# Decoding 64-bit weights in 8 pieces of 512 columns, one step per block

## The chip, the cores and the metric

The kernel runs on one core of one Trainium2 chip. The metric is the device time of one execution in microseconds (us). A core has a matrix engine (TensorE, PE in the profile; its weight loads are PEld), a vector engine (VectorE, DVE), an activation engine (ScalarE, ACT), a general engine (GpSimd, POOL) and a queue engine (SyncE, SP), from which this kernel issues all its transfers. They run side by side and wait for each other by semaphores. Each works through its own instructions strictly in the order in which the program lists them.

## The reference

Three stages follow each other on an input `x` of 8 batches x 3072 points x 256 features:

```python
X = rfft(x, axis=1)                       # stage 1: spectrum of every batch
Yr = Xr @ w_r - Xi @ w_i + b_r            #   complex mix of the features
Yi = Xr @ w_i + Xi @ w_r + b_i
y = irfft(soft_threshold(Yr, Yi, 0.01))
logits = y @ phi                          # stage 2: soft mixture, 8 experts x 4 slots
slots = softmax_over_points(logits).T @ y
z = softmax_over_slots(logits) @ relu(slots @ w1) @ w2   # expert by expert
h = z @ w_in                              # stage 3: 256 -> 1024 -> 256
u = h * softmax(h)
out = (layer_norm(u) * g_ln) @ w_out
```

`w_in` (256 x 1024) and `w_out` (1024 x 256) are products of a float32 array and a NumPy float64 scalar, so they arrive as 64-bit floats. The chip's engines work on 32-bit values. So the kernel takes each 64-bit number as two 32-bit integers, `lo` and `hi`, and builds the float32 from them with integer operations on VectorE.

## The kernel before

**Stages.** Phase 1 handles the spectrum, the mix and the slot sums of all batches. Phase 2 runs the experts and then the third stage over 192 tiles of 128 points. The change touches phase 1 alone.

**Blocks.** The main loop of phase 1 goes over 96 blocks: 8 batches of 12 groups of frequencies, `i = 12 b + t`. One turn of the loop lists, in this order:

1. `s1_next`: one part of the first transform stage of the next batch, in the first nine blocks of a batch. TensorE writes `s`, ScalarE copies it to `asb`, ScalarE and GpSimd split the next chunk of `x` into a high and a low part (`xsplit`, L224 on ScalarE, L225 on GpSimd). The result goes to DRAM (`ad`) and comes back as `apt`.
2. a `tick()`
3. `stage2` of block i + 1: four groups of matmuls into `xps`, two ScalarE copies (L285, L286), then VectorE's `xsum` (L287) and `xl` (L288). In blocks with even t, the load of a later `apt` is put on a list of delayed steps here.
4. a `tick()`, then `s1_next` and the transposes of block i - 2, then a `tick()`
5. `mix` of block i: matmuls into `pb` and `pa`, then VectorE's L329, L330 and L332, then GpSimd's L333, which finishes the soft threshold.
6. `stage2s` of block i + 1 (ScalarE L302, VectorE L303), then a `tick()`

**The narrow path.** Everything else of phase 1 (logits, the maxima, the softmaxes, the slot sums) is a chain of small steps. A step calls `after(n, fn)` to have the next one listed n ticks later, and `tick()` lists the steps that are due. There are four ticks in a block.

**The decoding.** `decode` lists the load of one piece, 128 partitions x 256 numbers of 8 bytes, into `raw` (L623). It hands ten VectorE operations (L630 to L639) to the delayed list, one per tick, the first one seven ticks later. Two ticks behind the last comes `dec_out`, a store of the 256 float32 columns into `win_dram` or `wout_dram` (L646). The tiles `raw`, `da`, `db` and `dm` exist once each. There are 16 pieces, and the loop starts one at the end of every fifth block (i = 4, 9, ..., 79). So the ten operations of the piece started at the end of block i lie behind the L303 of block i + 2 (the first), in blocks i + 3 and i + 4, and at the first tick of block i + 5 (the last). Counted from one L329 to the next, three stretches in a row hold operations of a piece, and the next two hold none.

**Where the results are needed.** The decoded weights are read back from DRAM at the end of phase 1 (`wo`, L133) and in phase 2 (`wi`, L811).

Of the kernel before, what the change touches and what calls it, by code (L numbers as in the profile page):

```python
# [8 lines left out]
F32 = mybir.dt.float32  # L9
F32R = mybir.dt.float32r  # L10
I32 = mybir.dt.int32
I64 = mybir.dt.int64
AF = mybir.ActivationFunctionType
ALU = mybir.AluOpType
# [4 lines left out]

# how many quarters of a block later each step of the narrow path is issued  # L20
LAG = dict(
    csoft_last=16, head=4, split0=3, load_x=3, a_out=0, qt=5, qtr=3, e2=3, r_x=2, inv1=3, mx=0, ltr=1, maxt=2, maxb=4,
    dsub=0, dexp=2, csoft=5, fwd1=4, rescale=3, rexp=3, csoft2=3, csoft3=5, c_x=4, c_out=1, dtr=3, d_x=3, fwd2=4,
    sums4=0, slots=1, sums=4, dec=7,
)
# [7 lines left out]
def kernel(  # L33
# [40 lines left out]
    ones = glob.tile([128, 128], F32, name="ones")  # L74
# [22 lines left out]

    # w1 and some of w2 in halves of 4 KB, the first ones where the chunks of x have been;
    # the rest of w2 in quarters where the spectra of the last batches have been
    w1t, w2t = {}, {}  # L100
# [35 lines left out]

    # ------------------------------------------------------------------ spectrum
    def phase1(pl: ExitStack, pr_: ExitStack):
# [25 lines left out]
        d2_sb = k_p.tile([128, 24, 128], F32, name="d2_sb")  # L164
        # [-(wr + wi) | wi - wr | wr]
        wc_h = k_p.tile([128, 2, 768], F32R, name="wc_h")
# [7 lines left out]

        # steps of the narrow path are put off by quarters of a block, so that what they wait for has ended
        heap = []
# [11 lines left out]

        # x loads and the first transform stage
        xt = {}  # L190
# [76 lines left out]
        def stage2(b, t):  # L267
            q, tq = divmod(t, 4)
            a = apt[b, q, tq // 2]
            ps = psx.tile([128, 2, 2, 2, 64], F32, name="xps", tag="xps")  # L270
            for gp in range(2):
                for dh in range(2):
                    mm(
                        ps[:, dh, :, gp, :],
                        a[:, gp, tq % 2, dh * 128:(dh + 1) * 128],
                        d2_sb[:, 8 * q + 2 * tq + gp, :].rearrange("p (c j) -> p c j", c=2),
                    )
            hi = xt_p.tile([128, 2, 2, 128], F32R, name="xh", tag="xh")
            lo = xt_p.tile([128, 2, 2, 128], F32R, name="xl", tag="xl")
            xi = xt_p.tile([128, 2, 128], F32, name="xi", tag="xi", bufs=1)  # L280
            sm_ = xt_p.tile([128, 2, 128], F32, name="xsum", tag="xsum", bufs=1)
            sh = xt_p.tile([128, 2, 128], F32R, name="sh", tag="sh")
            sl = xt_p.tile([128, 2, 128], F32R, name="sl", tag="sl")
            psv = ps.rearrange("p a c g j -> p a c (g j)")
            ACT.activation(out=xi, in_=psv[:, :, 1, :], func=AF.Copy)  # L285
            ACT.activation(out=hi, in_=psv, func=AF.Copy)  # L286
            DVE.tensor_tensor(out=sm_, in0=psv[:, :, 0, :], in1=xi, op=ALU.add)  # L287
            DVE.tensor_tensor(out=lo, in0=psv, in1=hi.bitcast(F32), op=ALU.subtract)  # L288
            if t == 0:
                # the first slot holds the two real frequencies: wr alone acts on both  # L290
                xd = xt_p.tile([128, 2, 1], F32, name="xd", tag="xd", bufs=1)
                DVE.tensor_tensor(out=xd, in0=xi[:, :, 0:1], in1=psv[:, :, 0, 0:1], op=ALU.subtract)
                DVE.tensor_copy(out=sm_[:, :, 0:1], in_=psv[:, :, 0, 0:1])
                DVE.tensor_copy(out=xd_h[:, :, 0:1], in_=xd)
                DVE.tensor_tensor(out=xd_l[:, :, 0:1], in0=xd, in1=xd_h[:, :, 0:1].bitcast(F32), op=ALU.subtract)
                for z in (hi, lo):
                    DVE.tensor_copy(out=z[:, :, :, 0:1], in_=zero4)
            xhl[b, t] = (hi, lo, sh, sl, sm_)
# [101 lines left out]

        # (part, n2) x (g, s) to (part, g) x (n2, s): one 32 x 32 block for each slot
        def r_x(b, z):
# [77 lines left out]

        # the running maximum of each column, and what it makes of the sums so far and of this batch's
        def rescale(b):
# [28 lines left out]

        # slots to the partitions; the points (row j, 8 m + a) in the order (a, j, m)
        def c_x(b, c, z):
# [76 lines left out]

        # the mean of g * w_out over the features
        def gmean(z):
# [26 lines left out]

        # decoding the 8 byte weights  # L620
        def decode(src, dst):
            raw = raw_p.tile([128, 256], I64, name="raw", tag="raw")
            SP.dma_start(out=raw, in_=src)  # L623
            v = raw.bitcast(I32).rearrange("p (n two) -> p n two", two=2)
            lo, hi = v[:, :, 0], v[:, :, 1]
            a = raw_p.tile([128, 256], I32, name="da", tag="da")
            c = raw_p.tile([128, 256], I32, name="db", tag="db")
            m = raw_p.tile([128, 256], I32, name="dm", tag="dm")
            ops = [
                lambda: DVE.tensor_scalar(out=a, in0=hi, scalar1=3, scalar2=0x7FFFFFF8, op0=ALU.logical_shift_left, op1=ALU.bitwise_and),  # L630
                lambda: DVE.scalar_tensor_tensor(out=a, in0=lo, scalar=29, in1=a, op0=ALU.logical_shift_right, op1=ALU.bitwise_or),
                lambda: DVE.scalar_tensor_tensor(out=a, in0=hi, scalar=_s32(0x80000000), in1=a, op0=ALU.bitwise_and, op1=ALU.bitwise_or),
# [3 lines left out]
                lambda: DVE.tensor_scalar(out=c, in0=a, scalar1=_s32(0xFF800000), scalar2=None, op0=ALU.bitwise_and),  # L636
                lambda: DVE.tensor_scalar(out=m, in0=lo, scalar1=0x1FFFFFFF, scalar2=None, op0=ALU.bitwise_and),
                lambda: DVE.scalar_tensor_tensor(out=c.bitcast(F32), in0=m, scalar=2.0**-52, in1=c.bitcast(F32), op0=ALU.mult, op1=ALU.mult),
                lambda: DVE.tensor_tensor(out=a.bitcast(F32), in0=c.bitcast(F32), in1=a.bitcast(F32), op=ALU.add),  # L639
            ]  # L640
            for k, op in enumerate(ops):
                after(LAG["dec"] + k, op)
            after(LAG["dec"] + len(ops) + 1, dec_out, dst, a.bitcast(F32))

        def dec_out(dst, f):
            SP.dma_start(out=dst, in_=f)  # L646

        # constants
        dft = sm_p.tile([96, 96], F32, name="dft", tag="qt_sb", bufs=2)
# [88 lines left out]
        decs = []  # L738
        for k in range(2):
            for h in range(4):  # L740
                decs.append((w_in[128 * k:128 * k + 128, 256 * h:256 * h + 256], win_dram[128 * k:128 * k + 128, 256 * h:256 * h + 256]))
        for k in range(8):
            decs.append((w_out[128 * k:128 * k + 128], wout_dram[128 * k:128 * k + 128]))

        for i in range(B * NT):
# [4 lines left out]
            if i + 1 < B * NT:  # L750
                stage2(*divmod(i + 1, NT))
                if t % 2 == 0:
                    k = i // 2 + 2
# [11 lines left out]
            tick()  # L765
            if decs and i % 5 == 4:
                decode(*decs.pop(0))
        st_transpose(B - 1, NT - 2)
# [10 lines left out]

    # ------------------------------------------------------------------ experts and the second block  # L780
    def phase2(p2: ExitStack, pw: ExitStack):
# [6 lines left out]

        # the slots' weights of a third of a batch, the same in the four groups of partitions
        def load_c(b, h):  # L790
# [11 lines left out]

        # the slots: the column groups added up, turned over
        ps = pt.tile([128, 2, 32], F32, name="pslt", tag="pt")
# [10 lines left out]

        # experts: four at a time in the column groups
        so = t_p.tile([128, 2, D], F32, name="so")
# [46 lines left out]
        for fh in range(2):  # L864
            for dh in range(2):
                mm(pg[fh], sot[:, dh].rearrange("p k s -> p (k s)"), wi[:, dh, 512 * fh:512 * fh + 512], dh == 0, dh == 1)
        # rows: high part twice, then low part twice
        for fh in range(2):
# [17 lines left out]

        # rows: high, low, high, low parts of the weights of 4 tiles
        def pieces(j):
# [13 lines left out]

        # the negated first product
        def hmat(i):
# [61 lines left out]

        # sum of (F u - sum u)^2
        def vari(i):
# [17 lines left out]

        # (F^3 (sum e + 1e-9)^2 1e-6 + variance sum) ** -0.5
        def rstd(j, k):
# [7 lines left out]
        def outp(i):  # L996
# [9 lines left out]
            if j == NG - 1:  # L1006
                # nothing left to wait for: each tile on its own
                rstd(j, slice(k, k + 1))
# [57 lines left out]

# [1 line left out]
def _consts():  # L1068
# [114 lines left out]
```

## Time and profile before

| | |
|---|---|
| three runs | 1517.56, 1522.68, 1522.99 us; median 1522.68 us |
| the profiled execution | 1519.0 us from its first to its last instruction; no other time is recorded for it |
| blocks 0 to 95 | L329 of block 0 at 43.8 us, of block 95 at 636.6 us |
| VectorE busy, whole span | 1267.1 us (83%) |
| TensorE busy, whole span | 1432.5 us (94%) |
| decoding operations | 160 on VectorE, 16 loads of 256 KB, 16 stores of 128 KB |

The span runs from the first instruction to the last. It lies among the three runs. Busy times are sums over one engine, and the engines overlap, so they don't add up to the span. A row of the trace names the line of the kernel, the engine, the operation, and its output and inputs by the program's names.

### The profile page before, as it was taken

Reading aid. Unit: us, or ns where it says so; the run is one execution under the profiler, and the core shown is the slowest. Engines: PE = TensorE matmul, PEld = TensorE weight load, DVE = VectorE, ACT = ScalarE, POOL = GpSimd, SP = SyncE. Lnnn points to the kernel's source line nnn. Section 1 sums busy time; section 2 is a strip of 40 time slices with the busy share of each in tenths; the row PEclk is TensorE's granted clock in tenths of the full one; section 3 lists DMA queues with packets and bytes.
Section 4 is the critical chain, followed back from the end, with each engine's and each line's share of the span. In section 5 each row is a group of like instructions: output and inputs, shape, how many; then the busy total and the mean of one; then the engine's idle time right before and its main releaser. Section 6 shows DMA issues by size and latency. Waiting matters only on the chain.

```text
span 1519.0 us, 31798 instructions
## 1 busy us (share of the span) xinstructions
PE 1432.5 (94%) x12300; PEld 1299.6 (86%) x12300; DVE 1267.1 (83%) x1981; ACT 1064.7 (70%) x2169; POOL 669.0 (44%) x703
## 2 busy tenths in 40 slices
PE   6998889989989999977999999999999999999999
PEld 3887777878778778745999999999999999999998
DVE  6698879998989898845888888888888888888886
ACT  5655564655555553423888888888888888888887
POOL 5545554645464543332334433433443344334432
PEclk8999999999999999988999999999999999999999
DMA  9955363626454551194111111111111111111001
GB/s 269 280 146 166 93 180 86 188 80 178 112 161 124 157 178 57 26 336 145 43 43 56 51 49 43 57 42 43 43 59 54 43 46 53 43 42 57 29 29 43
DMA packets 81383, 149.17 MB, mean 98 GB/s; under 512 B 9360, under 2 KB 46992, under 8 KB 81232
## 3 DMA queue, kind: packets, MB, share of 16 engines
q1 hardware_dynamic: 81232, 147.15, 31.3%
q8 instruction: 96, 1.57, 0.4%
q14 instruction: 55, 0.45, 0.1%
HBM read 91.55 MB, written 55.57 MB: 97 GB/s over the span
## 4 chain that ended last, share of the span: by engine, by line
PE 70%; DVE 17%; DMA 5%; issue 4%; ACT 2%; POOL 2%; SPq 0%; DVEq 0%; ACTq 0%; POOLq 0%
PE po L86 36%; PE pu L89 11%; PE hps L86 6%; PE pb L86 4%; PE s L86 3%; PE pm L86 3%; PE xps L86 2%; DMA xc<-in_x_dram 2%; DVE yb L330 2%; PE pa L86 2%; DVE yb L329 1%; DVE xl L288 1%; DVE sl L303 1%; DVE dm_sb L559 1%; DVE dm L634 1%
## 5 line engine op out<-in xcount | busy, mean ns | idle before, releaser
L923 DVE TENSOR_REDUCE st<-hps 128x1 f32<-128x1024 f32 x192 | 235.1, 1225 | 119.2 <-PE hps L86 119.2
L333 POOL TENSOR_TENSOR s<-yb,s 128x512 f32<-128x512 f32 x95 | 132.3, 1393 | 263.7 <-DVE s L332 227.0
L964 DVE TENSOR_TENSOR ul<-pu,uh 128x512 fp32r<-128x512 f32 x384 | 246.5, 684 | 0.8 <-ACT uh L956 0.8
L938 DVE SCALAR_TENSOR_TENSOR u<-hps,e 128x1024 f32<-128x1024 f32 x192 | 233.3, 1215 | 2.1 <-ACT e L930 2.1
L86 PE MATMUL po<-gw_h,uh 128*128 128x256 f32 x1536 | 230.3, 293 | 0.0
L973 ACT ACTIVATE sq<-u,st 128x1024 f32<-128x1024 f32 x192 | 224.4, 1169 | 0.0
L930 ACT ACTIVATE e<-hps,st 128x1024 f32<-128x1024 f32 x192 | 213.1, 1110 | 2.9 <-DVE st L923 2.9
L86 PE MATMUL po<-gw_l,uh 128*128 128x256 f32 x1536 | 213.5, 282 | 0.0
L86 PE MATMUL po<-gw_h,ul 128*128 128x256 f32 x1536 | 212.9, 280 | 0.0
L956 ACT ACTIVATE uh<-pu 128x512 fp32r<-128x512 f32 x384 | 208.7, 603 | 2.7 <-PE pu L89 2.7
L89 PEld LDWEIGHTS pu<-ident,u 128*128 128x128 f32 x1536 | 179.8, 140 | 26.0 <-DVE ul L964 0.6
L89 PE MATMUL pu<-ident,u 128*128 128x128 f32 x1536 | 199.9, 273 | 0.0
L86 PEld LDWEIGHTS po<-gw_h,ul 128*128 128x128 f32 x1536 | 196.2, 189 | 0.0
L86 PEld LDWEIGHTS po<-gw_h,uh 128*128 128x128 f32 x1536 | 195.7, 190 | 0.0
L86 PEld LDWEIGHTS po<-gw_l,uh 128*128 128x128 f32 x1536 | 195.6, 189 | 0.0
L225 POOL TENSOR_TENSOR x<-xc,x 96x512 fp32r<-96x512 f32 x120 | 161.9, 1360 | 37.1 <-ACT x L224 35.5
L1017 POOL TENSOR_TENSOR os<-osb,st 128x1024 f32<-128x1024 f32 x47 | 89.1, 1895 | 180.9 <-issue 173.2
L1012 ACT ACTIVATE osb<-po 128x256 f32<-128x256 f32 x188 | 72.2, 384 | 113.9 <-PE po L86 113.9
L898 POOL TENSOR_TENSOR c<-ct,c 32x512 fp32r<-32x512 f32 x96 | 123.2, 1283 | 6.7
L86 PE MATMUL hps<-gst,c 128*128 128x512 f32 x384 | 120.0, 394 | 5.8 <-DVE u L938 4.3
L993 POOL TENSOR_TENSOR st<-st 128x4 f32<-128x4 f32 (+1 forms) x51 | 10.1, 198 | 255.1 <-ACT sq L973 255.0
L86 PE MATMUL s<-x,df_h 96*96 96x512 f32 x240 | 105.6, 442 | 17.6 <-ACT asb L251 6.0
(191 smaller groups left out, 2693.5 us busy)
## 6 DMA issues: line engine op xcount, KB each, us to landing
apt<-ad SPq DMA_DIRECT2D x96, 256.0 KB, 4.1
out_dram<-os SPq DMA_DIRECT2D x47, 512.0 KB, 2.6
xc<-in_x_dram SPq DMA_DIRECT2D x56, 384.0 KB, 3.9
ad<-asb SPq DMA_DIRECT2D x56, 384.0 KB, 3.5
ct<-c_dram SPq DMA_DIRECT2D x96, 128.0 KB, 2.7
wt<-in_moe_w_dram SPq DMA_DIRECT2D x21, 512.0 KB, 9.3
ws<-in_moe_w_dram SPq DMA_DIRECT2D x22, 256.0 KB, 5.8
xc<-in_x_dram SPq DMA_DIRECT2D x16, 192.0 KB, 5.0
```

The costliest lines, as they stand in the source:

```text
L86: PE.matmul(out=out, lhsT=lhsT, rhs=rhs, start=start, stop=stop)
L89: PE.transpose(out=out, in_=in_, identity=ident[0:k, 0:k])
L225: POOL.tensor_tensor(out=lo, in0=t, in1=hi.bitcast(F32), op=ALU.subtract)
L333: (DVE if (b, t) == (B - 1, NT - 1) else POOL).tensor_tensor(out=s, in0=yb, in1=s, op=ALU.subtract)
L898: POOL.tensor_tensor(out=c4[z], in0=src[z], in1=c4[z].bitcast(F32), op=ALU.subtract)
L923: DVE.tensor_reduce(out=st[:, 0, k:k + 1], in_=hps[i], op=ALU.min, axis=AX.X)
L930: ACT.activation(out=e, in_=hps[i], func=AF.Exp, bias=st[:, 0, k:k + 1], scale=-1.0, accum_out=st[:, 1, k:k + 1])
L938: DVE.scalar_tensor_tensor(out=u, in0=hps.pop(i), scalar=1.0, in1=et.pop(i), op0=ALU.mult, op1=ALU.mult, accum_out=st[:, 2, k:k + 1])
L956: ACT.activation(out=uh[:, 4 * hf:4 * hf + 4, :], in_=ut[i, hf], func=AF.Copy)
L964: DVE.tensor_tensor(out=ul[:, 4 * hf:4 * hf + 4, :], in0=ut.pop((i, hf)), in1=uht[i][0][:, 4 * hf:4 * hf + 4, :].bitcast(F32), op=ALU.subt ...
L973: ACT.activation(out=sq, in_=ut.pop(i), func=AF.Square, bias=st[:, 2, k:k + 1], scale=-float(DFF), accum_out=st[:, 3, k:k + 1])
L1017: POOL.tensor_tensor(out=os2, in0=o, in1=q, op=ALU.mult)
```

## The change

The weights are decoded in 8 pieces of 128 x 512 numbers. A piece of `w_out` holds two groups of 128 rows. `raw` is now 4 KB per partition, and the three work tiles are 2 KB each.

A piece takes eight VectorE operations. The two that moved the top three bits of `lo` into the result and masked them out of `lo` are gone. The operation that adds the low part now takes all of `lo`, read as an unsigned integer.

The delayed list is no longer used for the decoding. `dec_step` is called once per block from i = 4 on, right behind `stage2`, and lists one operation. Its first call lists the load of the first piece alone. Behind the eighth operation of a piece, the same call lists the store of the piece and the load of the next. So piece n (0 to 7) has its operations in blocks 5 + 8n to 12 + 8n, and the last operation lies in block 68.

```diff
         def decode(src, dst):
-            raw = raw_p.tile([128, 256], I64, name="raw", tag="raw")
-            SP.dma_start(out=raw, in_=src)
...
+            raw = raw_p.tile([128, 512], I64, name="raw", tag="raw")
+            a = raw_p.tile([128, 512], I32, name="da", tag="da")
...
+            lo = raw.bitcast(U32).rearrange("p (n two) -> p n two", two=2)[:, :, 0]
...
+            SP.dma_start(out=r, in_=src)
...
-                lambda: DVE.scalar_tensor_tensor(out=a, in0=lo, scalar=29, in1=a, op0=ALU.logical_shift_right, op1=ALU.bitwise_or),
...
-                lambda: DVE.tensor_scalar(out=m, in0=lo, scalar1=0x1FFFFFFF, scalar2=None, op0=ALU.bitwise_and),
-                lambda: DVE.scalar_tensor_tensor(out=c.bitcast(F32), in0=m, scalar=2.0**-52, in1=c.bitcast(F32), op0=ALU.mult, op1=ALU.mult),
+                lambda: DVE.scalar_tensor_tensor(out=c.bitcast(F32), in0=lo, scalar=2.0**-52, in1=c.bitcast(F32), op0=ALU.mult, op1=ALU.mult),
                 lambda: DVE.tensor_tensor(out=a.bitcast(F32), in0=c.bitcast(F32), in1=a.bitcast(F32), op=ALU.add),
-            ]
-            for k, op in enumerate(ops):
-                after(LAG["dec"] + k, op)
-            after(LAG["dec"] + len(ops) + 1, dec_out, dst, a.bitcast(F32))
+                lambda: dec_out(dst, f),
+            ])
+
+        def dec_step():
+            if not dec_ops and decs:
+                decode(*decs.pop(0))
+                return
+            if dec_ops:
+                dec_ops.pop(0)()
+                if len(dec_ops) == 1:
+                    dec_ops.pop(0)()
+                    if decs:
+                        decode(*decs.pop(0))
...
             if i + 1 < B * NT:
                 stage2(*divmod(i + 1, NT))
+                if i > 3:
+                    dec_step()
                 if t % 2 == 0:
...
             tick()
-            if decs and i % 5 == 4:
-                decode(*decs.pop(0))
```

## Rows read from the trace of the kernel before

**Rows 1.** The page: two engines' busy time, and the chain that ended last

```profile
PE 1432.5 (94%) x12300; PEld 1299.6 (86%) x12300; DVE 1267.1 (83%) x1981; ACT 1064.7 (70%) x2169; POOL 669.0 (44%) x703
...
PE 70%; DVE 17%; DMA 5%; issue 4%; ACT 2%; POOL 2%; SPq 0%; DVEq 0%; ACTq 0%; POOLq 0%
```

**Rows 2.** Busy time by stage: stretch, its length, then each engine's busy time

```profile
200.00:300.00 100.00, 91.65 (x882) 79.09 (x881) 92.80 (x159) 59.87 (x134) 55.18 (x41) 0.98 0.52 146
400.00:500.00 100.00, 90.48 (x861) 76.35 (x859) 90.80 (x164) 55.28 (x124) 50.38 (x37) 0.98 0.41 117
760.00:1519.00 759.00, 755.52 (x6139) 731.48 (x6137) 638.14 (x896) 644.44 (x1260) 309.93 (x415) 1.00 0.13 46
```

**Rows 3.** The same, twelve stretches of two blocks without decoding operations, and their sum

```profile
core 0: us, PE busy (x) PEld busy (x) DVE busy (x) ACT busy (x) POOL busy (x), PEclk, DMA share, GB/s
...
251.18:264.68 13.50, 13.03 (x128) 10.33 (x127) 12.35 (x30) 6.87 (x16) 7.27 (x5) 1.00 0.18 55
283.64:292.26 8.62, 8.62 (x91) 7.97 (x93) 8.21 (x15) 6.74 (x15) 6.19 (x6) 1.00 0.91 245
314.97:325.89 10.92, 10.88 (x104) 9.64 (x96) 9.86 (x17) 6.94 (x18) 4.62 (x3) 1.00 0.53 158
...
482.65:496.06 13.41, 11.99 (x130) 9.03 (x130) 12.47 (x26) 6.44 (x14) 5.51 (x4) 1.00 0.35 109
...
549.83:560.86 11.03, 11.03 (x141) 10.21 (x141) 9.47 (x18) 6.86 (x16) 4.86 (x4) 1.00 0.78 258
sum 141.86, PE 135.68 PEld 116.76 DVE 110.33 ACT 90.11 POOL 79.29; mean PE 11.31 PEld 9.73 DVE 9.19 ACT 7.51 POOL 6.61
```

**Rows 4.** The same, sum over the twelve stretches of three blocks between them

```profile
sum 258.17, PE 230.39 PEld 197.10 DVE 249.18 ACT 138.66 POOL 125.97; mean PE 19.20 PEld 16.43 DVE 20.76 ACT 11.55 POOL 10.50
```

**Rows 5.** VectorE operations by line: durations in ns, least, median and greatest

```profile
L630 DVE TENSOR_SCALAR da<-raw x16: 1367/1380/1397, 74.4 to 563.1; 128x256 int32<-128x256 int32 x16
L632 DVE SCALAR_TENSOR_TENSOR da<-raw,da x16: 396/418/1201, 78.1 to 565.8; 128x256 int32<-128x256 int32 x16
L637 DVE TENSOR_SCALAR dm<-raw x16: 261/280/289, 84.9 to 576.1; 128x256 int32<-128x256 int32 x16
L639 DVE TENSOR_TENSOR da<-db,da x16: 358/932/1507, 88.8 to 581.9; 128x256 f32<-128x256 f32 x16
```

**Rows 6.** VectorE groups by line and shape: sum in us, mean in ns

```profile
L329 DVE TENSOR_TENSOR yb<-pb,bias 128x512 f32<-128x512 f32 x96 | 65.5, 682 | 18.5 <-PE pb L86 16.9 <-POOL x L225 0.6 <-POOL dt_sb L530 0.5
L332 DVE TENSOR_SCALAR s<-yb 128x512 f32<-128x512 f32 x96 | 42.6, 443 | 3.9
L303 DVE TENSOR_TENSOR sl<-xsum,sh 128x256 fp32r<-128x256 f32 x96 | 42.0, 437 | 2.3 <-ACT sh L302 2.3
```

**Rows 7.** The timeline around one L634: start in us, duration in us, engine

```profile
302.50 1.39 POOL L333 TENSOR_TENSOR s<-yb,s 128x512 f32<-128x512 f32 x1 [2.88 <-DVE s L332]
302.67 1.38 DVE L634 TENSOR_SCALAR dm<-db 128x256 int32<-128x256 int32 x1
```

**Rows 8.** The timeline at the ends of the first and last of 66 L288

```profile
59.97 1.30 POOL L225 TENSOR_TENSOR x<-xc,x 96x512 fp32r<-96x512 f32 x1
60.15 0.68 DVE L288 TENSOR_TENSOR xl<-xps,xh 128x512 fp32r<-128x512 f32 x1
...
481.54 2.02 POOL L496 TENSOR_TENSOR c_sb<-lg_sb,rm 96x1024 f32<-96x1024 f32 x1 [1.49 <-DVE rm L494]
482.05 0.67 DVE L288 TENSOR_TENSOR xl<-xps,xh 128x512 fp32r<-128x512 f32 x1
```

**Rows 9.** The queue: issue times of loads and stores (ns), landing times (us)

```profile
L623 SPq DMA_DIRECT2D raw<-in_moe_w_in_dram x8: 423/458/1367, 59.7 to 283.7; - x8
...
DMA to landing us min/median/max: 2.7/4.6/8.1
...
L646 SPq DMA_DIRECT2D win_dram<-da x8: 319/337/759, 89.3 to 313.6; - x8
...
wt<-in_moe_w_dram SPq DMA_DIRECT2D x6, 512.0 KB, 7.0
```

More of the change, by code (lines that the diff above doesn't have):

```diff
@@ L12 @@
 I64 = mybir.dt.int64
+U32 = mybir.dt.uint32
 AF = mybir.ActivationFunctionType
@@ L23 @@
     dsub=0, dexp=2, csoft=5, fwd1=4, rescale=3, rexp=3, csoft2=3, csoft3=5, c_x=4, c_out=1, dtr=3, d_x=3, fwd2=4,
-    sums4=0, slots=1, sums=4, dec=7,
+    sums4=0, slots=1, sums=4,
 )
@@ L618, in sums @@
                 after(1, slots, b)
+        dec_ops = []
         def decode(src, dst):
-            raw = raw_p.tile([128, 256], I64, name="raw", tag="raw")
-            SP.dma_start(out=raw, in_=src)
+            raw = raw_p.tile([128, 512], I64, name="raw", tag="raw")
+            a = raw_p.tile([128, 512], I32, name="da", tag="da")
+            c = raw_p.tile([128, 512], I32, name="db", tag="db")
+            m = raw_p.tile([128, 512], I32, name="dm", tag="dm")
             v = raw.bitcast(I32).rearrange("p (n two) -> p n two", two=2)
[L625 to L629, printed above, removed]
+            hi = v[:, :, 1]
+            lo = raw.bitcast(U32).rearrange("p (n two) -> p n two", two=2)[:, :, 0]
+            r = raw if len(src.shape) == 2 else raw.rearrange("p (k d) -> p k d", k=2)
+            SP.dma_start(out=r, in_=src)
+            f = a.bitcast(F32) if len(src.shape) == 2 else a.bitcast(F32).rearrange("p (k d) -> p k d", k=2)
+            dec_ops.extend([
                 lambda: DVE.tensor_scalar(out=a, in0=hi, scalar1=3, scalar2=0x7FFFFFF8, op0=ALU.logical_shift_left, op1=ALU.bitwise_and),
-                lambda: DVE.scalar_tensor_tensor(out=a, in0=lo, scalar=29, in1=a, op0=ALU.logical_shift_right, op1=ALU.bitwise_or),
                 lambda: DVE.scalar_tensor_tensor(out=a, in0=hi, scalar=_s32(0x80000000), in1=a, op0=ALU.bitwise_and, op1=ALU.bitwise_or),
@@ L739, in phase1 @@
         for k in range(2):
[L740 to L743, printed above, removed]
+            for h in range(2):
+                decs.append((w_in[128 * k:128 * k + 128, 512 * h:512 * h + 512], win_dram[128 * k:128 * k + 128, 512 * h:512 * h + 512]))
+        for k in range(0, 8, 2):
+            z = slice(128 * k, 128 * k + 256)
+            decs.append((w_out[z].rearrange("(k p) d -> p k d", p=128), wout_dram[z].rearrange("(k p) d -> p k d", p=128)))
         for i in range(B * NT):
```

## Prediction

> **What bounds the kernel now.** I began with the page. TensorE is busy for 94% of the span and VectorE for 83%, and the chain that ended last lies 70% on TensorE and 17% on VectorE [rows 1]. Such shares are means over stages with different limits, so the second view is busy time by stage. In phase 2, from 760 us on, TensorE works 755.5 of 759 us [rows 2]; nothing there changes. In the middle of phase 1 both engines are near the top: TensorE 91.65 and 90.48 of 100 us, VectorE 92.80 and 90.80 [rows 2]. Two engines at 91% may mean that each bounds some of the blocks, so the third view separates them.
>
> The decoding comes in a rhythm of five blocks: three stretches from L329 to L329 hold its operations, two hold none. I took blocks 24 to 83. Sixty is a multiple of both five and twelve, so every place t of a batch falls equally often on each beat, and the two kinds of block differ by decoding alone. Twenty-four blocks without it last 141.86 us, 5.911 us each; VectorE works 110.33 us in them, 4.597 each and 78% of the time, TensorE 135.68 us, 96% [rows 3]. Thirty-six blocks with it last 258.17 us, 7.171 each; VectorE works 249.18 us, 97%, TensorE 89% [rows 4]. So VectorE sets the pace where there is decoding, and TensorE, or the chain through it, elsewhere. A piece stretches three blocks by 1.260 us each, 3.78 us in all. The same windows say how: a piece brings 249.18 - 36 x 4.597 = 83.7 us of VectorE work over 12 pieces, 6.97 us each; the 1.314 us per block in which VectorE would have idled take up 3 x 1.314 = 3.94, and the remaining 3.03 must show as time. 3.78 is seen.
>
> **Why the old operations are dear.** L637 takes 261 to 289 ns, and L630, also one input and 256 columns, never less than 1367 [rows 5]. L630, L634 and L638 are listed at the last tick of a block, behind L332, whose end releases GpSimd's L333. The timeline shows the consequence: L333 runs from 302.50 to 303.89, and L634, begun at 302.67, ends at 304.05, just behind it [rows 7]. So an operation of this kind beside a GpSimd operation lasts until that one ends.
>
> The page "SBUF — State Buffer" of the Trainium skill, section "Who interferes with whom", states this as an exclusive lock: a tensor_scalar in a two-port mode, or a VectorE operation with two inputs in SBUF, and a GpSimd operation that reads SBUF block each other whole, in order of issue. The rule also cuts the other way: a decoding step that comes first would hold up GpSimd; that is the second rival below. By the row alone only the VectorE wait of 1.1 us counts.
>
> **The change part by part.**
>
> *Removed: the old decoding.* All 16 pieces go: 16 x 3.78 = 60.5 us less on the path. This applies the mean of twelve pieces to all.
>
> *Added: 64 operations of 512 columns.* Four are tensor_scalar; L332, that form at 512, takes 443 ns [rows 6]. It reads adjacent words, while two of the new ones read every other word as L637 does; L637's 280 at 256 columns [rows 5] shows no penalty. Three are scalar_tensor_tensor: L632 takes 418 at 256 [rows 5], and 256 more columns cost 682 - 437 = 245 ns by L329 against L303 [rows 6], so 663. One is a tensor_tensor: 358 at the least for L639 [rows 5], plus 245, 603. Together 4 x 443 + 3 x 663 + 603 = 4364 ns a piece, 546 an operation. Reading `lo` as unsigned has no row; nothing dearer than the 663 of its neighbours is assumed.
>
> To this comes waiting for GpSimd. At the new place, the end of L288, I read for 66 blocks (5 to 70, by the L288 in them) how long a GpSimd operation still ran. The first of these L288 ends at 60.83 with 0.44 us of L225 left, the last at 482.72 with 0.84 us of L496 left [rows 8]; with VectorE's next start some 0.07 us before the recorded end, 33 of 66 are covered at all, and the mean over all 66 is 0.34 us. The floor is 0, the ceiling 1.1 us, as for L630 [rows 5]. I take 0.34: 0.89 us an operation, 57 us of VectorE work in all, against 16 x 6.97 = 112.
>
> *How much of 0.89 us is on the path.* A block without decoding leaves VectorE 1.314 us, so on average it fits. The idle time is uneven, though. Of the twelve two-block stretches five have less than 2 x 0.89 = 1.78 us: 1.15, 0.41, 1.06, 0.94 and 1.56 [rows 3]. They lack 0.63, 1.37, 0.72, 0.84 and 0.22, 3.78 us over 24 blocks, 0.16 a block. That is too kind, since idle time need not lie where the step is. The old response is the other end: 3.78 us of time per 6.97 us of work, 0.54, times 0.89, 0.48 a block. I take the middle, 0.32: 64 x 0.32 = 20.5 us, with 10 and 31 as ends; the whole 57 is a rival's.
>
> *Moved: the reload.* Before, a piece's load had over two blocks to land. Now the store and the next load are listed behind the last step, and the first step of the next piece is listed one block later. It needs the new `raw`, and, since it writes `da`, the end of the store. On the queue the store is issued in 0.34 us and the load in about 0.43 [rows 9]. The old 256 KB loads land in 2.7, 4.6 and 8.1 us (least, median, greatest), and 512 KB of another tensor in 7.0 [rows 9]; at the 117 to 146 GB/s of these stretches [rows 2], 256 KB more take 1.8 to 2.2 us if they get that whole rate, less if the mean leaves room. I estimate 6.2 us. The step is due a block of 6.2 us later, less its predecessor's own 0.66, so about 5.5. VectorE waits 0.34 + 0.43 + 6.2 - 5.5 = 1.5 us, of which the 0.4 us left idle absorb a part: 1.1 us, eight times, 9 us. The first load stands alone in front of block 5, in batch 0, and is counted as one of the eight. Floor: 2.7 + 1 + 0.77 comes before 5.5, nothing. Ceiling: 8.1 + 2 + 0.77 - 5.5 = 5.4 us each, 43 in all.
>
> Behind the waiting step on VectorE stand the L329, L330 and L332 of its block and L303, behind L332 GpSimd's L333. TensorE can still run that block's mix, as its inputs were made one block earlier, but the next mix needs `pb` emptied by L329. That is why an absorbed part is credited and a hidden whole is not.
>
> *The queue.* The store now waits on SP for the eighth operation, and the load behind it goes out at once. Behind both stand the `apt` loads listed at the next tick, at most one step late, for a tile whose `stage2` comes three blocks on. So nothing is added for them. The cover is those blocks; without it, seven delays of about one step, 0.9 us, would cost 6 us. Bytes are the same, in half as many transfers.
>
> *Ends earlier.* The last operation lies in block 68, not 84. This is contained in the sum, which removes all old work and adds 64 operations.
>
> **The sum.** The profiled execution has a span of 1519.0 us and no separate time; the median of the runs is 1522.7, 3.7 more, which I leave outside the change. 1522.7 - 60.5 + 20.5 + 9 = 1491.7, about 1491 us; in terms of the span, 1488.
>
> **The rivals.**
>
> *Hidden whole.* If the steps fall into idle time and no load is late, only the 60.5 us remain: 1462. For it: 1.314 us idle a block against 0.89. Against it: the five tight stretches, and the ceiling of the loads.
>
> Beside it stands the rule in "Perfetto Trace Analysis" of the Trainium skill, section "Identifying the Most-Contended Engine", that matmul busy time is a poor measure and weight-load busy time a better one. By it TensorE would have 116.76 of 141.86 us, 82%, and the undecoded block would not be at its floor; a block at VectorE's 4.597 + 0.89 = 5.49 us would take the 64 blocks a further 64 x 0.42 = 27 us down, to 1435. This trace speaks against it only in that blocks with 78% VectorE still last 5.9 us.
>
> *The cover is gone.* If a step that starts first holds GpSimd back, L225 and L333 come late, and with them the next part of the first stage. Then each step costs its 0.89 us even where VectorE idles: 1522.7 - 60.5 + 57 + 9 = 1528, within 0.5% of before. Against it: GpSimd is only 55% busy at 200 to 300 us and 50% at 400 to 500 [rows 2].
>
> *TensorE is the floor everywhere.* If TensorE at 91% were the limit, VectorE's relief would be worth nothing: 1522. Against it: blocks without decoding are 1.26 us shorter at the same TensorE work [rows 3, 4].
>
> *Slower: the reload sets the pace.* Eight waits must give back 60.5 - 20.5 = 40 us, and 7.6 more for 0.5%, so over 6.0 us each on the path, a landing of about 11 us or more. At 8 us each: 1522.7 - 60.5 + 20.5 + 64 = 1547. For it: three of the eight loads (blocks 12, 36 and 60) fall on t = 0, where the next batch's transfers begin; one stretch without decoding shows the transfer engines 91% busy [rows 3]. Against it: no old load took over 8.1 us [rows 9].
>
> **Chances.** 0.5% is 7.6 us, about what a measurement of this kernel can tell from no change. The forecast has 0.70, hidden whole 0.13 (0.03 of it below 1458), cover gone 0.06, TensorE 0.04, the reload 0.07. Faster by over 0.5%: the first two, 0.83. Within it: 0.10. Slower: 0.07. The forecast's own range follows from 10 to 31 us for the steps and 0 to 24 for the waits: 1472 to 1517. To hold 8 in 10 I extend it down past hidden whole and leave the tail of the waits and the three slower cases out: 1458 to 1515.
>
> **What would show it.** VectorE's busy time falls by about 112 - 57 = 55 us; less than 30 would mean that waits for GpSimd are commoner. The new tensor_scalars should be near 0.44 us and the two-input ones near 0.66, half of them lengthened. Blocks 24 to 68 should last 6.2 us, blocks 69 to 83 5.9. The first operation of a piece should start with 1 to 2 us of idle time put down to the load or the store. If those idle times are over 6 us, the fourth rival holds; if blocks 69 to 83 last as long as before, the third does.

## The result and the profile after

The changed kernel takes 1477.99 us, the median of four runs (1475.65 to 1480.34), against 1522.84 us before in the same comparison. The ratio is 0.9721, with a 95% interval of 0.970 to 0.9743: 2.8% or 45 us faster. The profiled execution took 1476.49 us with a span of 1474.7 us.

Nearly all of it is won in phase 1. L330, which is L329 of the kernel before one line further down, comes in block 95 at 593.4 us (before: 636.6) and in block 0 at 42.1 (43.8). So 41.5 of the 44.3 us between the two spans lie between blocks 0 and 95. Another 1.7 us lie ahead of block 0, where neither kernel has decoded anything, and can't be put down to the change. From the page, the lines that answer to [rows 1]:

```profile
PE 1422.3 (96%) x12300; PEld 1293.8 (88%) x12300; DVE 1192.1 (81%) x1885; ACT 1065.2 (72%) x2169; POOL 671.9 (46%) x703
...
PE 76%; DVE 11%; DMA 7%; issue 3%; ACT 2%; POOL 1%; SPq 0%; DVEq 0%; ACTq 0%; POOLq 0%
```

VectorE works 75 us less, and its share of the chain falls from 17% to 11%, while TensorE's rises from 70% to 76%. The decoding operations of the changed kernel, by line and shape (VectorE's groups: busy us, mean ns, then idle time in front and what ended it), to be read against [rows 5, 6]:

```profile
L641 DVE SCALAR_TENSOR_TENSOR da<-da,dm 128x512 int32<-128x512 int32 x8 | 9.6, 1202 | 0.0
L644 DVE TENSOR_TENSOR da<-db,da 128x512 f32<-128x512 f32 x8 | 6.7, 836 | 0.0
L638 DVE SCALAR_TENSOR_TENSOR da<-raw,da 128x512 int32<-128x512 int32 x8 | 6.3, 789 | 0.0
L637 DVE TENSOR_SCALAR da<-raw 128x512 int32<-128x512 int32 x8 | 6.0, 753 | 6.2 <-DMA raw<-in_moe_w_in_dram 3.1 <-DMA raw<-in_moe_w_out_dram 3.1
L640 DVE TENSOR_SCALAR dm<-db 128x512 int32<-128x512 int32 x8 | 5.9, 740 | 0.0
L643 DVE SCALAR_TENSOR_TENSOR db<-raw,db 128x512 f32<-128x512 uint32 x8 | 5.5, 683 | 0.0
L642 DVE TENSOR_SCALAR db<-da 128x512 int32<-128x512 int32 x8 | 4.8, 595 | 0.0
L639 DVE TENSOR_SCALAR db<-raw 128x512 int32<-128x512 int32 x8 | 3.5, 442 | 0.0
```

They add up to 48.3 us, a mean of 755 ns over 64. The ten old groups add up to 137.7 us over 160 operations; half of that lies in three of the ten:

```profile
L638 DVE SCALAR_TENSOR_TENSOR db<-dm,db 128x256 f32<-128x256 int32 x16 | 24.1, 1509 | 0.0
L634 DVE TENSOR_SCALAR dm<-db 128x256 int32<-128x256 int32 x16 | 22.1, 1380 | 0.0
L630 DVE TENSOR_SCALAR da<-raw 128x256 int32<-128x256 int32 x16 | 22.1, 1380 | 0.0
```

In the changed kernel the first operation of a piece waits for its load, 6.2 us in all.

The operations of the changed kernel by line, with least, median and greatest duration:

```profile
L637 DVE TENSOR_SCALAR da<-raw x8: 427/639/1280, 63.2 to 401.6; 128x512 int32<-128x512 int32 x8
L638 DVE SCALAR_TENSOR_TENSOR da<-raw,da x8: 677/682/1118, 68.1 to 408.3; 128x512 int32<-128x512 int32 x8
L639 DVE TENSOR_SCALAR db<-raw x8: 417/418/578, 74.8 to 415.3; 128x512 int32<-128x512 int32 x8
L644 DVE TENSOR_TENSOR da<-db,da x8: 658/856/1060, 97.3 to 445.9; 128x512 f32<-128x512 f32 x8
```

The undisturbed operation is seen at the least or the median: 0.42 us for a tensor_scalar and 0.66 to 0.68 for those with two inputs. Busy time in blocks 24 to 68, which hold steps, and 69 to 83, which hold none (columns as in [rows 3]):

```profile
171.52:451.44 279.92, 268.15 (x2579) 231.56 (x2578) 228.38 (x422) 173.79 (x389) 161.13 (x118) 0.99 0.53 153
451.44:541.95 90.51, 88.71 (x874) 76.04 (x873) 71.74 (x141) 53.74 (x120) 45.70 (x34) 1.00 0.46 143
```

A block with a step lasts 279.92 / 45 = 6.22 us, and one without 90.51 / 15 = 6.03.

### The profile page after: what moved, and what is told of

The parts are those of the page before. It is cut to its first block, busy times and chain, and to the rows that moved or that the text cites. A ratio compares the mean times of both kernels' runs of the same rounds, so it can differ in the third digit from the quotient of the medians.

```text
span 1474.7 us, 31675 instructions
## 1 busy us (share of the span) xinstructions
PE 1422.3 (96%) x12300; PEld 1293.8 (88%) x12300; DVE 1192.1 (81%) x1885; ACT 1065.2 (72%) x2169; POOL 671.9 (46%) x703
## 4 chain that ended last, share of the span: by engine, by line
PE 76%; DVE 11%; DMA 7%; issue 3%; ACT 2%; POOL 1%; SPq 0%; DVEq 0%; ACTq 0%; POOLq 0%
PE po L87 37%; PE pu L90 11%; PE hps L87 6%; PE pb L87 6%; PE s L87 3%; PE pm L87 3%; PE xps L87 3%; PE pa L87 2%; DMA xc<-in_x_dram 2%; DMA ad<-asb 2%; PE sps L90 1%; DVE yb L330 1%; DVE yb L331 1%; DVE xl L289 1%; DVE dm_sb L560 1%
## 5 line engine op out<-in xcount | busy, mean ns | idle before, releaser
L334 POOL TENSOR_TENSOR s<-yb,s 128x512 f32<-128x512 f32 x95 | 132.2, 1391 | 223.5 <-DVE s L333 208.5
L226 POOL TENSOR_TENSOR x<-xc,x 96x512 fp32r<-96x512 f32 x120 | 164.8, 1381 | 41.2 <-ACT x L225 37.4
L252 ACT ACTIVATE asb<-s 96x512 f32<-96x512 f32 x112 | 66.7, 596 | 82.7 <-PE s L87 72.2
```

Of the source, the lines that this page charges most:

```text
L226: POOL.tensor_tensor(out=lo, in0=t, in1=hi.bitcast(F32), op=ALU.subtract)
L334: (DVE if (b, t) == (B - 1, NT - 1) else POOL).tensor_tensor(out=s, in0=yb, in1=s, op=ALU.subtract)
```

## The experiments

**The theory.** The old decoding cost time in two ways: 160 small operations, and places at which three in ten of them always stood beside a GpSimd operation. Eight pieces of 512 remove the first and the new place the second. What is left, some 22 us, is one step a block that VectorE cannot hold in its idle time, plus waits for loads. **Rivals:** size alone gives the gain and the place is worth nothing; place alone gives it; the decoding was hidden, so that the floor is near 1478.

Medians of runs on the same chip are compared. Before is 1519.9 us beside the first four runs below, 1520.4 beside the next four and 1520.7 beside the last four.

**One operation a piece.**

```diff
-            dec_ops.extend([
...
-                lambda: dec_out(dst, f),
-            ])
+            dec_ops.append(lambda: DVE.tensor_scalar(out=a, in0=hi, scalar1=0x007FFFFF, scalar2=0x3F000000, op0=ALU.bitwise_and, op1=ALU.bitwise_or))
+            dec_ops.extend([lambda: None] * 7)
+            dec_ops.append(lambda: dec_out(dst, f))
```

> The changed kernel with one VectorE operation a piece left instead of eight, in the same block as before the first of them; loads, stores and their places unchanged. Left out: the decoding itself (the weights of the third stage are other numbers). My sum: the steps cost 0.32 us a block, so 56 fewer give 18 us back: about 1460. Rival (the old decoding cost more than the 60.5 us that I took off, and the steps cost as I said or more): the floor is lower than 1522.7 - 60.5 = 1462 although loads and stores remain; by batch 6 of the changed kernel, which has no steps (70.0 us against 75.0 in batches 2 to 4), 0.42 us a block, about 1454. Rival (hidden whole): 1476 to 1478.

Measured: 1457.65 us (1454.36 to 1459.16), ratio 0.9591 (0.9567 to 0.9615), between the 1460 of the sum and the 1454 of the first rival. The floor lies below 1462, so hidden whole falls. The 20 us between 1458 and 1478 are the price of 56 steps together with most of the waiting for loads, which falls from 6.2 to 0.5 us in front of the one operation left:

```profile
L636 DVE TENSOR_SCALAR da<-raw 128x512 int32<-128x512 int32 x8 | 7.1, 882 | 0.5 <-DMA raw<-in_moe_w_in_dram 0.5
```

**The step at the end of the block.**

```diff
-                if i > 3:
-                    dec_step()
...
                 stage2s(*divmod(i + 1, NT))
+                if i > 3:
+                    dec_step()
```

> The changed kernel with the step (and the store and load behind the eighth) listed at the end of a block, behind L304, instead of behind the second transform stage. If the place makes the old operations dear (GpSimd's soft-threshold operation has just been released there), each step lasts some 1.4 to 1.8 us instead of 0.75, VectorE gets about 60 x 0.9 = 55 us more work, and half or so shows as time: 1495 to 1520. Rival (the place is worth nothing, it was fewer and longer operations that gained): within 5 us of the changed kernel.

Measured: 1504.3 us (1501.99 to 1506.6), ratio 0.9895 (0.9872 to 0.9917). The same 64 operations, and 26 us more than the changed kernel. Two of them by line, and then the timeline around L643:

```profile
L638 DVE SCALAR_TENSOR_TENSOR da<-raw,da 128x512 int32<-128x512 int32 x8 | 14.2, 1772 | 0.0
L640 DVE TENSOR_SCALAR dm<-db 128x512 int32<-128x512 int32 x8 | 12.1, 1514 | 0.0
```

```profile
301.10 1.28 POOL L226 TENSOR_TENSOR x<-xc,x 96x512 fp32r<-96x512 f32 x1 [0.27 <-ACT x L225]
...
306.62 1.39 POOL L334 TENSOR_TENSOR s<-yb,s 128x512 f32<-128x512 f32 x1 [2.48 <-DVE s L333]
306.80 1.77 DVE L643 SCALAR_TENSOR_TENSOR db<-raw,db 128x512 f32<-128x512 uint32 x1
307.98 1.74 POOL L226 TENSOR_TENSOR x<-xc,x 96x512 fp32r<-96x512 f32 x1
```

L638 takes 1772 ns here and 789 in the changed kernel. GpSimd's L334 ends at 308.01, and L643 ends 0.56 us later: it waited, then ran. All eight groups add up to 95.4 us against 48.3. GpSimd is held up in turn: the L226 that begins at 307.98, beside L643, takes 1.74 us, the one at 301.10 1.28. Over the whole execution the 39 L226 that begin while a decoding operation runs take 1.62 us on average, the other 81 take 1.33.

**New pieces in the old places**, one operation per tick, a piece every ten blocks.

```diff
...
+            for k, op in enumerate(ops):
+                after(7 + k, op)
+            after(7 + len(ops) + 1, dec_out, dst, f)
...
-                if i > 3:
-                    dec_step()
...
+            if decs and i % 10 == 4:
+                decode(*decs.pop(0))
```

> The pieces of 512 with eight operations, but listed as in the kernel before: one operation per tick through the delayed list, a piece every ten blocks. If size and count of the operations bring the gain: near 1478. If the place and the even spread do: the eight operations of a piece press into two blocks, two of them (the first and the fifth) behind L333 in GpSimd's shadow; by the old response of 0.54 us per us of work, with 8 x (4.4 + 2.2 + 1) = 61 us of work, 33 us against the 20.5 + 9 of the forecast: about 1480 to 1490. So this arm expects most of the gain from the size.

Measured: 1492.27 us (1489.95 to 1497.3), ratio 0.982 (0.9793 to 0.9847): 27.6 us of gain from size and count alone. That is most of the gain, as expected, but the time lies above both ranges that were given. The first and the fifth operation, listed behind L333 and L304, are the dearest, and the fourth goes undisturbed:

```profile
L641 DVE SCALAR_TENSOR_TENSOR da<-da,dm 128x512 int32<-128x512 int32 x8 | 14.2, 1780 | 0.0
L637 DVE TENSOR_SCALAR da<-raw 128x512 int32<-128x512 int32 x8 | 12.1, 1512 | 0.0
...
L640 DVE TENSOR_SCALAR dm<-db 128x512 int32<-128x512 int32 x8 | 3.4, 428 | 0.3
```

**Old pieces in the new place**, sixteen of 256 with ten operations, two per block.

```diff
...
                 stage2(*divmod(i + 1, NT))
+                if i > 3:
+                    dec_step()
+                    if i > 4:
+                        dec_step()
...
-            if decs and i % 5 == 4:
-                decode(*decs.pop(0))
```

> The old sixteen pieces of 256 with ten operations, listed behind the second transform stage, two per block in 80 blocks. If the place does it: operations near 0.28 to 0.42 us plus a wait for the first of the two, some 160 x 0.45 = 72 us of VectorE work instead of 112 to 138, 0.9 us a block: within 15 us of the changed kernel (1478 to 1493). If size and count do it: near 1510 or above. Sixteen reloads one block ahead of use, of half the size, are in either.

Measured: 1500.35 us (1496.53 to 1503.48), ratio 0.9867 (0.984 to 0.9894): 19.5 us of gain from the place alone, less than the 27 to 42 that the text allowed it and more than the rival's 1510 leaves, so neither expectation holds. The 160 operations still take 107.8 us, where 72 were expected. Size and place together would make 47.1 us if they added up; the change gives 42 to 45.

**The changed kernel again**, as the base for the next three.

> The changed kernel once more, as the base for the three runs beside it: 1476 to 1481.

Measured: 1477.9 us (1477.26 to 1478.91), ratio 0.9724 (0.9702 to 0.9746).

**An earlier load.**

```diff
+        dec_cm = [raw_p.tile([128, 512], I32, name=n, tag=n) for n in ("db", "dm")]
...
-            a = raw_p.tile([128, 512], I32, name="da", tag="da")
-            c = raw_p.tile([128, 512], I32, name="db", tag="db")
-            m = raw_p.tile([128, 512], I32, name="dm", tag="dm")
+            a = raw_p.tile([128, 512], I32, name="da", tag="da", bufs=2)
+            c, m = dec_cm
...
+                if len(dec_ops) == 2 and decs:
+                    decode(*decs.pop(0))
-                if len(dec_ops) == 1:
+                if len(dec_ops) % 9 == 1:
                     dec_ops.pop(0)()
-                    if decs:
-                        decode(*decs.pop(0))
```

> The changed kernel with a second da tile and the load of the next piece listed behind the seventh operation instead of the eighth, so one block earlier. If the 6.2 us in which VectorE waits for raw lie on the path as other VectorE time does (about 0.45 us per us): 2 to 4 us less than the changed kernel; by the 9 us of my sum, 9 less. Rival (the waits fall where VectorE had idled anyway): no difference.

Measured: 1474.3 us (1473.66 to 1475.45), ratio 0.970 (0.9678 to 0.9722). 3.6 us less than the base, and the two ranges don't touch. The wait is gone from the line:

```profile
L637 DVE TENSOR_SCALAR da<-raw 128x512 int32<-128x512 int32 x8 | 7.0, 875 | 0.0
```

So the reloads cost 3.6 us. (The second `da` tile also frees the first operation from the store of the piece before, but in the changed kernel all of the 6.2 us are put down to the load.) This is the fastest version with all of the work in it whose runs lie close together.

**Steps in the roomy blocks.**

```diff
                 if i > 3:
-                    dec_step()
+                    for _ in range(1 if i == 4 else (1, 2, 2, 1, 0, 2, 2, 0, 0, 0, 0, 0)[t]):
+                        dec_step()
```

> The changed kernel with the same 64 operations listed only in the blocks where, in the run with one operation a piece, VectorE idles over 1.4 us: t = 0 and 3 (one), 1, 2, 5 and 6 (two). None in t = 4 and 7 to 11, where it idles 0.1 to 1.2 us. If the steps cost what VectorE cannot hold in each block, most of the 20 us between 1458 and 1478 goes: 1460 to 1470. Rival (every us of decoding work costs some 0.45 us wherever it lies): 1476 to 1480.

Measured: 1489.01 us (1487.32 to 1494.06), ratio 0.9801 (0.9777 to 0.9824), 11 us slower than the base. It is a poor test of its theory. The idle times were read from L330 of block t to the next L330, and the step of turn t stands in front of L330 of block t, so in stretch t - 1: the steps fell on stretches 11, 0, 1, 2, 4 and 5, and stretch 4 is a tight one. Two steps a block also bring the first of a piece close behind its load:

```profile
L637 DVE TENSOR_SCALAR da<-raw 128x512 int32<-128x512 int32 x8 | 5.1, 634 | 22.5 <-DMA raw<-in_moe_w_out_dram 11.8 <-DMA raw<-in_moe_w_in_dram 10.7
```

22.5 us of waiting instead of 6.2: this is how the fourth rival of the prediction looks when it bites.

**No decoding.**

```diff
-            SP.dma_start(out=r, in_=src)
...
+            f = dec_z if len(src.shape) == 2 else dec_z.rearrange("p (k d) -> p k d", k=2)
+            dec_ops.extend([lambda: None] * 8)
+            dec_ops.append(lambda: dec_out(dst, f))
...
+        dec_z = raw_p.tile([128, 512], F32, name="dec_z")
+        POOL.memset(dec_z, 0.01)
```

> The changed kernel without the decoding: no loads of 64-bit pieces, no operations; the eight stores go out in their places from a constant tile. Left out: the decoding (the weights of the third stage are a constant). It gives the floor against which both removal and addition are read. If loads and queue cost nothing: 3 us below the run with one operation a piece, 1454 to 1457. If the loads cost by crowding the transfers of x and ad: under 1450.

Measured: 1455.34 us (1454.25 to 1456.22), ratio 0.9577 (0.9548 to 0.9605). That is 2.3 us below the run with one operation a piece, which has all the loads and eight operations; so the loads by themselves cost nothing that can be seen. Two of its batches, then 100 to 450 us of this kernel, of the changed one and of the one before (three fences, one view):

```profile
169.87:240.30 70.43, 70.43 (x693) 61.13 (x692) 54.46 (x103) 46.04 (x103) 41.65 (x31) 1.00 0.52 147
...
381.17:451.60 70.43, 70.43 (x693) 61.12 (x692) 54.42 (x103) 46.04 (x103) 41.58 (x31) 1.00 0.50 145
...
100.00:450.00 350.00, 350.00 (x3439) 303.49 (x3438) 269.74 (x508) 229.66 (x513) 206.89 (x155) 1.00 0.50 144
```

```profile
100.00:450.00 350.00, 336.72 (x3251) 290.39 (x3250) 287.00 (x527) 218.97 (x490) 202.88 (x149) 0.99 0.53 153
```

```profile
100.00:450.00 350.00, 318.50 (x2968) 273.77 (x2966) 312.36 (x545) 202.80 (x452) 188.01 (x138) 0.98 0.48 137
```

Without decoding TensorE never stops in this stretch, and the batches last the same to a hundredth of a microsecond: 5.87 us a block, set by TensorE with VectorE at 77%. Before, VectorE worked 42.6 us more of these 350 and TensorE stood still for 31.5; in the changed kernel it stands still for 13.3.

**Ten operations.**

```diff
+                lambda: DVE.scalar_tensor_tensor(out=a, in0=v[:, :, 0], scalar=29, in1=a, op0=ALU.logical_shift_right, op1=ALU.bitwise_or),
...
+                lambda: DVE.tensor_scalar(out=m, in0=v[:, :, 0], scalar1=0x1FFFFFFF, scalar2=None, op0=ALU.bitwise_and),
```

> The changed kernel with the two dropped operations put back: eight pieces of 512 with ten operations, one per block, the last in block 84. Sixteen more operations of about 0.68 and 0.44 us and their waits for GpSimd, some 12 us of VectorE work. At 0.45 us of time per us of work: 5 us more, 1482 to 1485. If they fall into idle time: no difference from the changed kernel (1478).

Measured: 1481.86 us (1479.09 to 1483.65), ratio 0.9747 (0.9722 to 0.9771). The two dropped operations are worth about 4 us of the 45. That is at the edge of what can be told here: the base of 1477.9 was measured on another chip (before 0.3 us apart), and the intervals of the two ratios overlap.

**The step in front of the second transform stage.**

```diff
-                stage2(*divmod(i + 1, NT))
                 if i > 3:
                     dec_step()
+                stage2(*divmod(i + 1, NT))
```

> The changed kernel with the step listed in front of the second transform stage instead of behind it, one edit. Without decoding VectorE idles 0.68 us a block in front of the stage's first VectorE operation and 0.44 in front of L330 (blocks 24 to 68). If idle time counts by its size: a few us less than the changed kernel, 1470 to 1476. Rival (at this place GpSimd's L334 and L226 are running, as for the old L631, L635 and L639 at 0.88 to 0.99 us for 256 columns): 1.2 to 1.4 us a step, 1485 to 1495.

Measured: 1477.4 us (1475.81 to 1481.43), ratio 0.9728 (0.9702 to 0.9754): no difference from the changed kernel, though neither expectation holds. An operation here is almost as dear as at the end of the block: 85.4 us for the 64, and 9.6 us of waiting for the load besides. Three lines of this kernel, then L288 of the changed one:

```profile
L288 DVE TENSOR_TENSOR xsum<-xps,xi 128x256 f32<-128x256 f32 x96 | 39.7, 414 | 27.2 <-ACT xh L287 26.6
...
L638 DVE SCALAR_TENSOR_TENSOR da<-raw,da 128x512 int32<-128x512 int32 x8 | 13.6, 1697 | 0.0
...
L637 DVE TENSOR_SCALAR da<-raw 128x512 int32<-128x512 int32 x8 | 7.8, 979 | 9.6 <-DMA raw<-in_moe_w_in_dram 5.8 <-DMA raw<-in_moe_w_out_dram 3.7
```

```profile
L288 DVE TENSOR_TENSOR xsum<-xps,xi 128x256 f32<-128x256 f32 x96 | 39.8, 415 | 64.8 <-ACT xh L287 63.6
```

The idle time in front of L288 falls from 64.8 to 27.2 us. That matches the 37 us by which the 64 operations are dearer here, most of it waiting for GpSimd. So these lie, at least in sum, in time in which VectorE otherwise waits for ScalarE, and the kernel takes no longer.

**Two slots, and no tight blocks**, both on the kernel with the early load.

```diff
...
-            if dec_ops:
+            if dec_ops and not (len(dec_ops) % 9 == 0 and i < dec_due[0]):
...
+                if i > 3 and t in (1, 2, 3, 4, 7):
+                    dec_step(i)
                 stage2(*divmod(i + 1, NT))
-                if i > 3:
-                    dec_step()
+                if i == 4 or i > 4 and t in (0, 1, 2, 3, 6, 9):
+                    dec_step(i)
```

> On the kernel with the early load: steps only where, without decoding, VectorE has over 0.3 us of idle time in that block and place: in front of the second transform stage in turns t = 1, 2, 3, 4 and 7 (VectorE waits there for ScalarE), behind it in t = 0, 1, 2, 3, 6 and 9 (it waits there for the mix). No first operation of a piece earlier than two turns behind its load. If a step costs only what its own place cannot hold: 1460 to 1468. Rival (the places in front collide with GpSimd's split of x and the waits outgrow the idle time): 1475 to 1485.

```diff
-                if i > 3:
+                if i > 3 and t not in (5, 8, 11):
                     dec_step()
```

> On the kernel with the early load (1474): all steps behind the second transform stage, none in turns t = 5, 8 and 11, whose stretches (4, 7 and 10) have no idle time in front of L330 without decoding. Three of twelve steps had cost their whole 0.75 us there. If the place decides: 64 x 3/12 x 0.5 = 8 us less, about 1466 to 1470. Rival (a step costs the same everywhere, and loses nothing by moving): 1474.

Measured: 1474.08 us with two slots (1469.33 to 1485.27, ratio 0.9706, 0.9675 to 0.9736) and 1477.63 without the tight blocks (1474.42 to 1484.27, ratio 0.973, 0.9703 to 0.9758). Neither betters the 1474.3 of the early load; the gain that the idle times promised did not come, and neither median lies in a range that was given. The runs spread widely, and they go with the granted clock of TensorE, averaged over an execution: with two slots 1485.27 us at 0.979 and 1469.33 at 0.988, without the tight blocks 1484.27 at 0.981 and 1474.42 at 0.986. The early load ran at 0.985 to 0.986 throughout, and at these clocks two slots took 1473.12 and 1475.04 us, no less.

## Why the prediction was right, point by point

The forecast of 1491 us was 13 us above the result, in the range and of the right sign. The mechanism was right: the old decoding cost time at its places beside GpSimd and by its number of operations, and part of the new one stays on the path. Of the 13 us some 5 lie in the removal, 5 in the reload and 1.5 in the steps; 2 more are the start, 1522.7 us where the kernel before took 1520.4 beside these runs. Its terms against the runs:

| term | forecast | measured | from |
|---|---|---|---|
| old decoding out | -60.5 | -65.0 | before 1520.4, no decoding 1455.34 |
| steps in | +20.5 | +19.0 | early load 1474.3, no decoding 1455.34 |
| reloads in | +9 | +3.6 | changed 1477.9, early load 1474.3 |
| sum | -31 | -42.4 | changed 1477.9, before 1520.4 |

**What bounds the kernel: right.** The beat of five blocks separated the two bounds. Decoded blocks were at VectorE's pace; the others, measured at 5.911 us [rows 3], stand at 5.87 without any decoding, where TensorE works without a pause. The 4.5 us by which the removal was mis-sized are largely this 0.04 us, over 80 blocks 3.3 us. The traces say the same: blocks 24 to 83 last 400.03 us before and 351.78 without decoding, 4.02 us a piece where 3.78 was read. That the beat came so close is partly luck, though. The two kinds of stretch do not differ by decoding alone: by [rows 3, 4] TensorE is busy 5.65 us in a stretch without decoding and 6.40 in one with it, and 54 matmuls begin in the one and 60 in the other, so some of TensorE's work had moved between them. For the same reason the rival of TensorE as the floor was answered wrongly with "the same TensorE work".

**Why the old operations are dear: right.** The run at the end of the block moves the step there, with the store and the load that go with its eighth operation, and makes an operation last 1491 ns instead of 755. The lock that the page "SBUF — State Buffer" of the Trainium skill describes in "Who interferes with whom" agrees, in both directions: L643 ended 0.56 us behind L334, and L226 was lengthened from 1.28 to 1.74 us.

**The price of an operation: right when undisturbed, too high for the wait.** Forecast were 443, 663 and 603 ns; seen are 417, 682 and 658. Reading `lo` as unsigned costs nothing (683). The wait for GpSimd came out at (48.3 - 8 x 4.37) / 64 = 0.21 us instead of 0.34, with 4.37 us for four of 417, three of 682 and one of 658. So the steps are 48 us of VectorE work and not 57. Part of the miss is in the reading: the trace before gives about this mean (0.35) where the same GpSimd line run twice in a row counts as one wait. Counting only the operation that runs at that moment, the 66 places give 0.28.

**How much is on the path: right in size, wrong in its reason.** 0.30 us a block against 0.32. The forecast read the price from how unevenly VectorE's idle time lies. Moving steps by that reading gained nothing, and the run in front of the stage shows that 37 us more of VectorE work can be free. Idle time on VectorE is no measure of what TensorE will wait for. What the steps cost is read on TensorE. Blocks 24 to 68 hold the same 2579 matmuls in the changed kernel (its row stands above) and in the one without decoding:

```profile
169.87:432.29 262.42, 262.42 (x2579) 228.59 (x2578) 200.27 (x376) 173.76 (x389) 157.52 (x118) 1.00 0.54 154
```

The changed kernel takes 17.5 us longer for them. In 11.8 of these TensorE stands still; for the other 5.7 its matmuls show as busy for longer, in part at a lower clock (below). What ended the 11.8 us, in the changed kernel (us in total, times, longest):

```profile
PE s L87 <- ACT asb L252: 4.4, 3, 2.0
PE pm L87 <- DVE acc L590: 2.7, 3, 1.0
PE pm L90 <- ACT lt_sb L422: 2.5, 3, 1.2
PE pb L87 <- DVE yb L330: 1.2, 3, 0.7
PE pm L87 <- DVE dm_sb L560: 1.0, 3, 0.5
```

Copies of ScalarE ended 6.9 us of it and results of VectorE 4.9. So TensorE mostly does not wait for VectorE itself; by which chain a step delays these copies was not traced.

**A term that the sum does not have: TensorE's clock.** Three rows of the kernel before:

```profile
239.84 0.63 PE L86 MATMUL pb<-wc_h,xl 128*128 128x256 f32 x4
...
244.87 1.09 PE L86 MATMUL pb<-wc_h,xh 128*128 128x256 f32 x4 [2.37 <-DVE yb L329]
...
246.61 1.06 PE L86 MATMUL pb<-wc_h,xl 128*128 128x256 f32 x4
```

TensorE stands still for 2.37 us until 244.87. From 245.04 to 248.45 its granted clock is 0.50 (1.2 GHz), and four matmuls take 1.06 us that take 0.63 at 1.00 (2.4 GHz). Between blocks 0 and 95 the profiled execution before has six such stretches of 3.4 us, the changed kernel two, the one without decoding none. Beside each of the eight TensorE has a pause, of 1.2 to 3.5 us. The run in front of the stage has pauses too (up to 1.6 us) and no such stretch, so which pauses bring one is open. An estimate from these rows: a stretch loses 3.4 x (1 - 0.63 / 1.06) = 1.4 us, so four fewer give some 5.5. Runs of like mean clock bound it: four executions before at 0.982 took 1514.16 to 1518.76 us, one of the changed kernel at 0.981 took 1480.34. So 34 to 38 of the 42 to 45 us stand without the clock, and at most the rest goes with it. The run without decoding (0.986 to 0.988) holds this gain too, so the removal's 65.0 contains it.

**The reload: the term that was most mis-sized.** Loads land in 4.3, 5.2 and 7.2 us (least, median, greatest) where 6.2 was estimated, so six of eight first steps waited, 6.2 us in all or 0.8 a piece where 1.5 had been forecast, and they cost 3.6 us on the path, not 9.

**The rivals.** Hidden whole: refuted, 22.6 us are left of the decoding. Cover gone: GpSimd is held back as described, but the price stayed at 0.30 us a step, not 0.89. TensorE as the floor everywhere: it is the floor of the undecoded block alone. The reload: real, but 3.6 us where this rival needed 48. The page "Perfetto Trace Analysis" of the Trainium skill, in "Identifying the Most-Contended Engine", would have put TensorE at its weight loads, 303.49 of 350 us or 87%, with room left (it also goes by the share of peak arithmetic, which wasn't worked out here); with no decoding matmuls are busy for all 350 and the trace shows no wait of TensorE there. The 1435 us that the forecast worked out by that rule lie below the 1455 that are left without any decoding. Here the busy time told the pace.

**What was said to show it.** Blocks with a step 6.22 us (6.2 said), without 6.03 (5.9); without any decoding the same fifteen blocks last 89.36 us, 5.96 each. 29 of the 64 operations were lengthened (half said). VectorE's busy time fell by 75 us, not 55. It is 1150.8 us without decoding, so the old decoding made up 116.3 of it (112 forecast) and the new one 41.3 (57 forecast). Of the 16 us between these two, 9 are the shorter waits for GpSimd; the other 7 are the difference between the 48.3 us to which the 64 records add up and the 41.3 by which the engine's busy time grew. Neighbouring records overlap: the forecast itself put VectorE's next start some 0.07 us before the recorded end of L288.

## What to carry to other kernels

Where work comes in a beat, compare the stretches with it and without it: that difference predicted the gain from removal within 5 us of 65, where busy shares of 91% on two engines said nothing. Check that the other engines do the same work in both kinds of stretch; here they did not quite. An operation's price belongs to its place as much as to its size: the same 64 operations took 48, 85 or 95 us in three places of one block. Judge what they cost by the engine that sets the pace, since 85 us, largely in time that VectorE had to wait anyway, cost no more than 48 elsewhere. And look at the granted clock before putting a spread of runs, or a gain, down to the program's order alone.

## What had not been expected

Size and place gave 27.6 and 19.5 us apart and 42.4 together, and the response of time to VectorE's decoding work (the idle time in front of it included) is far from constant: (1520.4 - 1455.3) / 138.6 = 0.47 us per us before, (1477.9 - 1455.3) / 55.4 = 0.41 in the changed kernel run again, and (1477.4 - 1455.3) / 95.0 = 0.23 in front of the stage.
